# Sliding-window attention and a two-layer MLP: weights of a head in 192 columns, products with v as 128x64 and 64x64 tiles

## The chip, the cores and the metric

The kernel runs on one core of one Trainium2 chip. The metric is the device time of one execution in microseconds (us), as the median of several runs. A profiled execution has a time of its own; its span is what lies between its first and its last instruction. TensorE (PE in the profile) multiplies, VectorE (DVE) and ScalarE (ACT) work element by element, GpSimd (POOL) and SyncE (SP) mainly issue DMAs here. SBUF is the working memory with 128 partitions, PSUM the memory that TensorE writes.

## What is computed

```python
# q, k, v: (8, 8, 576, 64) = batch, heads, sequence, head_dim
def _attn_ref(q, k, v):
    window, scale = 128, 1.0 / np.sqrt(D)
    scores = scale * np.matmul(q, k.transpose(0, 1, 3, 2))
    rel = pos[:, None] - pos[None, :]
    slopes = 2.0 ** (-8.0 * (np.arange(H, dtype=np.float32) + 1) / H)
    bias = slopes[:, None, None] * (-np.abs(rel).astype(np.float32))[None, :, :]
    mask = (rel >= 0) & (rel < window)
    scores = np.where(mask, scores + bias[None], -1000000000.0)
    attn = softmax of scores over the keys
    return np.matmul(attn, v)

def _moe_ref(x, g_ln, w_ch1, w_ch2):   # x: (8, 576, 512), the heads side by side
    xn = (x - mu) / np.sqrt(var + 1e-06) * g_ln
    ch = np.maximum(xn @ w_ch1, 0.0) @ w_ch2      # 512 -> 2048 -> 512
    return (x + ch).astype(np.float32)
```

A query sees itself and the 127 keys before it. So a block of 128 queries needs two blocks of 128 keys, and of the 256 keys in them each query needs 128.

## The kernel before

**Blocks and order.** The batches are taken two at a time (four pairs, p = 0 to 3). The 576 tokens of a batch are four blocks of 128 and a tail of 64. A pair has nine slots: slot 2i + b is block i of its batch b, and slot 8 (`T`) is the two tails together, one batch on 64 partitions each. `order` lists the 36 slots; n is the place in it. Slots 0 and 1 see only their own keys, slots 2 to 7 those of slot blk - 2 and their own, slot 8 those of slots 6 and 7 and its own. The MLP works on groups of slots (`GROUPS`: 2, 2, 2, 2, then seven of 4).

**Two streams in one order.** `steps` (L740 to L794) is the list of attention steps. The MLP is a set of generators (`mlp1`, `mlp2`, `mlp2_seven`, `mlp1_last`, `mlp2_last`), and `weave_at` runs a given number of attention steps after given units of them. Each engine executes its instructions in the order in which they were written this way. For n from 8 on (L772 to L794) a slot has four steps: the first holds the masks and the products with v of slot n and one call of `attend` for slot n + 2 (or, if slot n + 1 is a tail, the tail's own-key call), the second the other calls, the third and fourth masks, squares and DMA transposes.

**Loads.** POOL issues the loads of q, k, v and the weights in the order of `loads` (L291 to L311), at most up to a given place (`load_until`). `load_v` (L283) makes one DMA per slot, two for a tail, into one of ten v buffers `vext`, [128 tokens, 8 heads, 64 + a column of ones]. From n = 13 on q and k are loaded as they lie (`load_natural`, L258; k one DMA for each batch, q two, even and odd tokens apart) and turned by DMA transposes that SP issues (`turn_natural`, L370). Before that, q and k are loaded with two tokens in a row (`load_qk`), turned by TensorE (`transposed`) and copied out of PSUM by DVE and ACT in `turn`, `turn_first` and `copy_second`. k's copy puts the tokens back in order and so writes with a stride; q's copy leaves the even tokens first and the odd ones behind, and writes in a row. Outputs are stored to even and odd rows by two DMAs (`store`, L1216).

**Scores.** `attend` (L469) computes transposed scores, keys on partitions and queries along columns, with K = 64 (head_dim) and 64 keys at a time, so each product uses a 64x64 quarter of the array; the two heads of a head pair hp use the two halves of the rows (j), the key halves c the two halves of the columns. `seen` (L443) leaves out those 64 keys by 64 queries that the window excludes, except in the first pair (`SEEN`). A call for two head pairs fills a pair of PSUM banks, [128 keys, 2, 2, 2 key blocks, 128 queries]; ACT takes the exponential (L504) into `probs`, 1024 columns at a time, and DVE multiplies by the decay mask (`masks`, L516). The masks `m_full`, `m_ends`, `m_tail` hold exp(-slope x distance), or 0 outside the window; ACT makes them from tables of distances (`decay`, L149). For slots 0 and 1 of the first pair TensorE adds the distances instead (`add_distances`). The tail has three calls: two for the keys of slots 6 and 7, one (`tail_attend`) for its own keys.

**Products with v.** In `values_at_once` (L571) each head and key block is one product with the weights [128 keys, 128 queries] stationary and 65 columns of `vext` moving, L579; for slots 2 to 7 that is 16 products, for the tail 24, for slots 0 and 1 eight. Slots 4 to 7 of the first pair do the same in two halves of four heads (`values`, L540, products at L550). The 65th column gives the sum of the weights. DVE divides by it (L587, L588; L558, L559), then `centre` subtracts the mean and the block goes into the MLP.

**The start.** The first steps turn the first slot by TensorE, with products on constants (`warm`) between. SP loads `first_tables` (the identity and two tables of distances) and the gains, POOL the first q and k, then v of slots 0 and 1, q and k of slot 2, the first quarter of w1, v of slots 2 and 3, the other quarters of w1 and two of w2.

Of the kernel before, what the change touches and what calls it, by code (L numbers as in the profile page):

```python
# [32 lines left out]
BY_DMA = SEEN = 8  # L33
# [38 lines left out]
def tables():  # L72

    key = np.arange(P)[:, None]
    query = np.arange(P)[None, :]

    def far(rel, ok=True):
        return np.where(ok & (rel >= 0) & (rel < WINDOW), rel, FAR)

    ends = [far(P + query - HALF * b - key, query // HALF == b) for b in range(2)]
    tail = far(query - key, query // HALF == key // HALF)
    evens_first = np.r_[0:P:2, 1:P:2]
    both = [far(P + query - key), far(query - key)]
    cols = [np.eye(P), *(m[:, evens_first] for m in both), *ends, tail]
    return np.concatenate(cols, axis=1).astype(np.float16)
# [3 lines left out]
def kernel(  # L93
# [21 lines left out]
    def pool(name, bufs, **kw):  # L115
# [22 lines left out]
    more_tables = consts.tile([P, 3 * P], FP16)  # L138
# [5 lines left out]
    m_full, m_ends = (  # L144
        consts.tile([P, H, 2 * P], FP16, name=f"m{i}", tag=f"m{i}") for i in range(2)
    )
    m_tail = consts.tile([P, H, P], FP16)

    def decay(m, heads=range(H)):  # L149

        n = m.shape[2]
        src = {id(m_full): first_tables[:, P:], id(m_ends): more_tables[:, 0 : 2 * P]}.get(
            id(m), more_tables[:, 2 * P :]
        )
        for h in heads:
            nc.scalar.activation(
                out=m[:, h, :],
                in_=src,
                func=AF.Exp,
                scale=-(2.0 ** (-8.0 * (h + 1) / H)),  # L160
            )
# [31 lines left out]
    def load_tables():  # L193
        nc.gpsimd.dma_start(out=more_tables, in_=tables_dram[:, 3 * P :])

    def slopes():

        for h in range(H):
            nc.vector.tensor_scalar(
                out=bias[:, h],  # L200
                in0=first_tables[:, 2 * P :],
# [56 lines left out]
    def load_natural(src, tag, p, i):  # L258
# [24 lines left out]
    def load_v(p, blk):  # L283
        vx = vext[(p * NSLOT + blk) % NV]
        for b, t0, n, p0 in spans(p, blk):
            nc.gpsimd.dma_start(  # L286
                out=vx[p0 : p0 + n, :, 0:D],
                in_=v[b, :, t0 : t0 + n, :].rearrange("h p d -> p h d"),
            )
# [59 lines left out]
    def turn(p, i, in_sc=False, copies=(nc.vector.tensor_copy, nc.scalar.copy)):  # L349
# [37 lines left out]
    def queries(p, i):  # L387
        t = turned_pool["q"].tile([P, 2, 2, HP, HALF], FP16, tag="q", name="q")
        turned["q", p, i] = t.rearrange("p b r h c -> p b h r c")
        return t  # L390

# [7 lines left out]
    def turn_first(b, copy):  # L399

        if b == 0:
            first_turned.extend((queries(0, 0), keys_tile("k", 0, 0)))
# [13 lines left out]
        nc.vector.tensor_copy(out=q[:, b], in_=ps[0])  # L416
        copy(out=k[:, b].rearrange("p h (c r) -> p r h c", r=2), in_=ps[1])
# [8 lines left out]
    def copy_second():  # L426

        q, k, ps = queries(0, 1), keys_tile("k", 0, 1), second_pair
        for t, b, copy in (
# [5 lines left out]
            dst = t[:, b] if t is q else t[:, b].rearrange("p h (c r) -> p r h c", r=2)  # L435
# [4 lines left out]
    def in_halves(t):  # L440
        return t if len(t.shape) == 3 else t.rearrange("p (r c) -> p r c", r=2)
# [880 lines left out]
```

## Time and profile before

| | |
|---|---|
| median of 3 runs | 308.59 us (308.33 to 309.37) |
| profiled execution | 307.95 us, span 306.2 us |
| granted TensorE clock | 0.993 of full speed |
| TensorE weight loads busy | 203.2 us (66%), beside the products |
| scores, L495 | 1088 products of 64x64 tiles |
| products with v, L579 and L550 | 480 and 64 of 128x128, 65 columns each |
| exponentials, L504 | 68 x 128x1024, 1.02 us each |
| masks, L516 | 66 x 128x1024, 0.68 us each |
| v loads, L286 | 40 issues on POOL, 34.1 us |
| natural q loads, L275 | 40 issues on POOL, 27.4 us |
| POOL's DMA queue | 103792 packets, 18.46 MB |
| HBM | read 36.90 MB, written 9.44 MB |

A row of the timeline gives the start of a run of like instructions, the time to the end of the last, the engine, the line of the kernel, the operation, what is written and read, the shape of the tile in the array, the moving operand and the count. TensorE's products overlap, so what a run costs is the distance from its start to the start of the next run. A row of waits names who waited for whom, the total, the number of times and the longest.

### The profile page before, as it was taken

How to read it: one execution, taken by the hardware profiler on the slowest of the kernel's cores; microseconds unless marked ns; L12 is line 12 of the kernel's file. 1: busy time of each engine (PE TensorE's matmuls, PEld its weight loads, DVE VectorE, ACT ScalarE, POOL GpSimd, SP SyncE). 2: the span in 40 equal slices, each digit the busy share in tenths (PEclk: the TensorE clock that was granted, in tenths of full speed). 3: DMA queues.
4: the chain of work that ended last, by engine and by line, in shares of the span. 5: the costliest groups of instructions: out<-in, count | busy, mean ns of one | idle time of the engine just before them, and what ended most of it. 6: DMA issues, size and time to landing. Idle time of an engine off the chain costs nothing.

```text
span 306.2 us, 9262 instructions
## 1 busy us (share of the span) xinstructions
PE 296.9 (97%) x3778; PEld 203.2 (66%) x3778; DVE 242.8 (79%) x646; ACT 181.7 (59%) x332; POOL 112.3 (37%) x153
## 2 busy tenths in 40 slices
PE   6899999999999999999999999999999999999994
PEld 2477755866755568646864686568656865698883
DVE  2588878779996799569967986798799878978983
ACT  5588776768966863675368635853586268506500
POOL 8933659763774372475107250760000000000000
PEclk9799999999999999999999999999999999999999
DMA  9999999999999999999999999999451043005014
GB/s 98 172 202 200 194 158 170 205 135 89 138 126 186 146 132 145 181 184 148 112 171 120 125 121 149 119 151 120 105 122 37 19 96 77 19 19 137 3 34 103
DMA packets 150074, 38.03 MB, mean 124 GB/s; under 512 B 140656, under 2 KB 145920, under 8 KB 150032
## 3 DMA queue, kind: packets, MB, share of 16 engines
q0 software_dynamic: 103792, 18.46, 96.0%
q1 hardware_dynamic: 45760, 18.60, 37.1%
q8 instruction: 29, 0.48, 0.7%
q10 hardware_dynamic: 480, 0.39, 0.5%
q14 instruction: 13, 0.11, 0.2%
HBM read 36.90 MB, written 9.44 MB: 151 GB/s over the span
## 4 chain that ended last, share of the span: by engine, by line
PE 91%; DMA 4%; ACT 1%; DVE 1%; POOL 1%; issue 1%; DVEq 0%; ACTq 0%; POOLq 0%
PE ps_m L832 35%; PE ps_s L1062 25%; PE ps_m L862 9%; PE ps_sc L495 6%; PE ps_sc L579 5%; PE ps_q L1141 4%; PE ps_x L956 3%; DMA q<-q 3%; DMA first<-in_k_dram 2%; PE ps_tr L343 1%; PE ps_warm L331 1%; POOL first L187 1%; PE ps_pv L550 1%; PE ps_tx L640 1%; PE ps_t L956 1%
## 5 line engine op out<-in xcount | busy, mean ns | idle before, releaser
L832 PE MATMUL ps_m<-xT,w1g 128*128 128x512 f16 (+1 forms) x512 | 103.7, 353 | 0.1
L848 ACT ACTIVATE ht_all<-ps_m 128x512 f16<-128x512 f32 (+1 forms) x143 | 71.5, 512 | 26.1 <-PE ps_m L832 24.0
L504 ACT ACTIVATE probs<-ps_sc 128x1024 f16<-128x1024 f32 x56 | 56.6, 1024 | 45.4 <-PE ps_sc L495 45.4
L832 PEld LDWEIGHTS <-w1g 128*128 128x128 f16 x512 | 47.7, 98 | 42.6 <-issue 0.3
L286 POOL DMA_DIRECT2D vx<-in_v_dram x40 | 34.1, 859 | 67.9 <-PE ps_sc L579 38.1
L1062 PE MATMUL ps_s<-w,s 128*128 128x256 f16 x384 | 43.8, 273 | 0.0
L1062 PEld LDWEIGHTS <-s 128*128 128x128 f16 x384 | 36.7, 98 | 4.7
L516 DVE TENSOR_TENSOR probs<-probs,m 128x1024 f16<-128x1024 f16 x56 | 36.9, 683 | 2.5 <-ACT probs L504 2.5
L1062 PE MATMUL ps_s<-w,ht_all 128*128 128x256 f16 x288 | 34.3, 273 | 0.0
L862 PE MATMUL ps_m<-w,ht_all 128*128 128x512 f16 x128 | 31.3, 380 | 0.0
L1062 PEld LDWEIGHTS <-ht_all 128*128 128x128 f16 x288 | 27.4, 98 | 4.9
L275 POOL DMA_DIRECT2D q<-in_q_dram x40 | 27.4, 697 | 6.0 <-DMA vx<-in_v_dram 2.2
L1083 DVE SCALAR_TENSOR_TENSOR o<-ps_s,rstd,x 128x256 f32<-128x256 f32 x48 | 21.0, 478 | 8.5 <-PE ps_s L1062 8.4
L882 DVE TENSOR_TENSOR s<-ht_all 128x1024 f16<-128x1024 f16 (+2 forms) x36 | 20.5, 571 | 7.9 <-ACT ht_all L848 6.7
L495 PE MATMUL ps_sc<-q,k 64*64 64x128 f16 (+1 forms) x1088 | 24.8, 212 | 0.6 <-ACT q L436 0.3
L495 PEld LDWEIGHTS <-k 64*64 64x64 f16 x1088 | 16.2, 108 | 13.2 <-issue 10.3
L588 DVE SCALAR_TENSOR_TENSOR x<-ps_sc,rec 128x512 f16<-128x512 f32 x32 | 22.1, 691 | 1.1
L272 POOL DMA_DIRECT2D k<-in_k_dram x20 | 17.9, 910 | 8.4 <-DMA k<-k 5.9
L664 ACT ACTIVATE junk<-xc 128x512 f16<-128x512 f16 x28 | 17.6, 628 | 5.7 <-DVE xc L620 5.6
L1083 DVE SCALAR_TENSOR_TENSOR o<-ps_s,rstd,o 128x256 f32<-128x256 f32 x36 | 15.7, 478 | 3.4 <-PE ps_s L1062 3.1
L579 PEld LDWEIGHTS <-probs 128*128 128x128 f16 x384 | 15.9, 98 | 3.6
L862 PEld LDWEIGHTS <-ht_all 128*128 128x128 f16 x128 | 11.1, 98 | 10.8
(117 smaller groups left out, 371.7 us busy)
## 6 DMA issues: line engine op xcount, KB each, us to landing
out_dram<-o SPq DMA_DIRECT2D x64, 128.0 KB, 2.5
vx<-in_v_dram POOLq DMA_DIRECT2D x32, 128.0 KB, 7.1
w<-in_moe_w_ch_dram POOLq DMA_DIRECT2D x8, 512.0 KB, 11.2
k<-in_k_dram POOLq DMA_DIRECT2D x30, 128.0 KB, 7.2
q<-in_q_dram POOLq DMA_DIRECT2D x48, 64.0 KB, 6.7
q<-in_q_dram POOLq DMA_DIRECT2D x10, 128.0 KB, 6.8
out_dram<-o SPq DMA_DIRECT2D x10, 64.0 KB, 1.9
k<-in_k_dram POOLq DMA_DIRECT2D x8, 64.0 KB, 7.7
```

What stands on the lines that cost most here:

```text
L275: nc.gpsimd.dma_start(out=t[half, b], in_=tokens.rearrange("h (c r) d -> r c h d", r=2)[r],)
L286: nc.gpsimd.dma_start(out=vx[p0 : p0 + n, :, 0:D], in_=v[b, :, t0 : t0 + n, :].rearrange("h p d -> p h d"),)
L495: nc.tensor.matmul(in_halves(ps[cols, j, n, t, :])[:, r, queries], kt[rows, hp, cols], in_halves(qt[rows, b, hp])[:, r, queries], start=no ...
L504: nc.scalar.activation(out=dst.rearrange("p (n j) q -> p j n q", j=2), in_=ps.rearrange("p j n t q -> p j n (t q)"), func=AF.Exp, scale=in ...
L516: nc.vector.tensor_tensor(out=dst, in0=dst, in1=mask, op=ALU.mult)
L579: nc.tensor.matmul(ps[:, h, 0 : D + 1], pr[:, h, t, :], vext[(p * NSLOT + o) % NV][:, h, :], start=(n == 0), stop=(n == len(terms) - 1),)
L588: nc.vector.scalar_tensor_tensor(out=x.rearrange("p (h d) -> p h d", h=H), in0=ps[:, :, 0:D], scalar=1.0, in1=rec.unsqueeze(2).broadcast_t ...
L832: nc.tensor.matmul(ps[:, 0:cols], w[:, kb, fb * P : (fb + 1) * P], xT[:, kb, 0:cols], start=(kb == 0), stop=(kb == NKB - 1),)
L848: nc.scalar.activation(out=ht[:, fb, :], in_=ps[:, 0:cols], func=AF.Relu)
L862: nc.tensor.matmul(sums[at], ht[:, fb, at * P : (at + 1) * P], w2[:, fb, :], start=(fb == 0), stop=(fb == NFB - 1),)
L1062: nc.tensor.matmul(ps[:, pair, :], lhs[:, fb, at : at + P], rhs[:, fb, :], start=(first and pair == 0 and fb == 0), stop=(fb == half - 1), ...
L1083: nc.vector.scalar_tensor_tensor(out=outs[at][:, cols], in0=ps[:, pair], scalar=rstd[:, n : n + 1], in1=(xs[p, blk] if fresh else outs[at] ...
```

## The change

The weights of a head for a slot with two key blocks take 192 columns in place of 256. A query of the first half of the block (early) needs all of the earlier block's second half, and parts of the earlier block's first half and of its own first half; one of the second half (late) needs all of its own first half, and parts of its own second half and of the earlier block's second half. The 192 columns are: all 128 earlier keys for the early queries (64 columns); 64 columns shared by two quarters, the own first half of the keys for the early queries on one half of the partitions and the earlier second half for the late queries on the other; the 128 own keys for the late queries (64 columns). The tail is put into 192 columns in the same way, with its own keys in the middle, so that it has two calls of `attend` and no third. For heads 4 to 7 the two halves of the partitions change places, in the scores, the masks and v.

`weigh` makes the products with v: for each head two of a 128x64 tile (all rows, 64 queries), then, all heads over again, two of a 64x64 tile for the middle columns. Slots 0 and 1 keep 128x128. `load_v` loads heads 0 to 3 as before, and heads 4 to 7 with the halves about, in two DMAs: three for a slot in place of one, four for a tail in place of two. Queries are in token order everywhere: q's copies write with a stride like k's, natural q is one DMA for each batch, and outputs are stored by one DMA for each slot, but for the last four. The scores in the first pair leave out what the window excludes, too. The masks' tables are now [identity, own and own turned about], [two and two turned about], [last and last turned about], of 96 KB each; SP loads the second right behind the first.

```diff
-BY_DMA = SEEN = 8
+BY_DMA = 8
...
+    early, late = query[:, :HALF], query[:, HALF:]
+    upper = key < HALF
+    def far(rel):
+        return np.where((rel >= 0) & (rel < WINDOW), rel, FAR)
+    own = far(query - key)
+    of_two = np.where(upper, early - key, P + late - key)
+    two = np.concatenate([far(P + early - key), far(of_two), far(late - key)], axis=1)
+    ahead = far(P + early - key)
+    last = np.concatenate([ahead, far(early - key % HALF), ahead], axis=1)
+    cols = [np.eye(P)]
+    for m in (own, two, last):
+        cols += [m, np.roll(m, HALF, axis=0)]
...
+    next_tables, more_tables = (
+        consts.tile([P, 6 * HALF], FP16, name=f"tables{i}", tag=f"tables{i}") for i in range(2)
+    )
...
-    m_full, m_ends = (
-        consts.tile([P, H, 2 * P], FP16, name=f"m{i}", tag=f"m{i}") for i in range(2)
+    m_two, m_last = (
+        consts.tile([P, H, 3 * HALF], FP16, name=f"m{i}", tag=f"m{i}") for i in range(2)
     )
-    m_tail = consts.tile([P, H, P], FP16)
-    def decay(m, heads=range(H)):
+    m_own = consts.tile([P, H, P], FP16)
+    def distances(m, h):
         n = m.shape[2]
-        src = {id(m_full): first_tables[:, P:], id(m_ends): more_tables[:, 0 : 2 * P]}.get(
-            id(m), more_tables[:, 2 * P :]
-        )
-        for h in heads:
+        src = {id(m_two): next_tables, id(m_last): more_tables}.get(
+            id(m), first_tables[:, P:]
+        )
+        return src[:, 2 * h // H * n : (2 * h // H + 1) * n]
...
-            if tag == "k":
-                nc.gpsimd.dma_start(out=t[:, b], in_=tokens.rearrange("h p d -> p h d"))
-            else:
-                for r, half in enumerate([slice(0, HALF), slice(HALF, P)]):
-                    nc.gpsimd.dma_start(
-                        out=t[half, b],
-                        in_=tokens.rearrange("h (c r) d -> r c h d", r=2)[r],
-                    )
+            nc.gpsimd.dma_start(out=t[:, b], in_=tokens.rearrange("h p d -> p h d"))
...
         vx = vext[(p * NSLOT + blk) % NV]
-        for b, t0, n, p0 in spans(p, blk):
-            nc.gpsimd.dma_start(
-                out=vx[p0 : p0 + n, :, 0:D],
-                in_=v[b, :, t0 : t0 + n, :].rearrange("h p d -> p h d"),
-            )
+        for heads, turned_about in ((slice(0, HP), False), (slice(HP, H), True)):
+            for b, t0, n, p0 in spans(p, blk):
+                tokens = v[b, heads, t0 : t0 + n, :].rearrange("h p d -> p h d")
+                if not turned_about:
+                    parts = [(p0, tokens)]
+                elif blk == T:
+                    parts = [(HALF - p0, tokens)]
+                else:
+                    parts = [(0, tokens[HALF:]), (HALF, tokens[:HALF])]
+                for at, src in parts:
+                    nc.gpsimd.dma_start(out=vx[at : at + src.shape[0], heads, 0:D], in_=src)
...
-            q = queries(p, i)
+            q = keys_tile("q", p, i)
             transposed("q", p, i, [t[:, 0] for t in ps])
             transposed("k", p, i, [t[:, 1] for t in ps])
             for b, copy in enumerate(copies):
-                copy(out=q[:, b], in_=ps[b][:, 0])
-                copy(out=k[:, b].rearrange("p h (c r) -> p r h c", r=2), in_=ps[b][:, 1])
+                for t, dst in enumerate((q, k)):
+                    copy(out=dst[:, b].rearrange("p h (c r) -> p r h c", r=2), in_=ps[b][:, t])
...
-        nc.vector.tensor_copy(out=q[:, b], in_=ps[0])
-        copy(out=k[:, b].rearrange("p h (c r) -> p r h c", r=2), in_=ps[1])
+        for t, src, copy in ((q, ps[0], nc.vector.tensor_copy), (k, ps[1], copy)):
+            copy(out=t[:, b].rearrange("p h (c r) -> p r h c", r=2), in_=src)
...
+    lower, upper, whole = slice(0, HALF), slice(HALF, P), slice(0, P)
+    def seen(blk):
         if blk == T:
-            batches = [slice(0, 1), slice(1, 2)]
-            return [(c, batches[c if o == T else t], every) for c in range(2)]
-        if o == blk:
-            return [(0, both, every), (1, both, second)]
-        return [(1, both, every), (0, both, first)]
+            turns = [(6, c, lower, 0) for c in range(2)] + [(7, c, upper, P) for c in range(2)]
+            return turns + [(T, 0, lower, HALF), (T, 1, upper, HALF)]
+        if blk < 2:
+            return [(blk, c, whole, 0) for c in range(2)]
+        return [
+            (blk - 2, 1, whole, 0),
+            (blk - 2, 0, lower, 0),
+            (blk, 1, upper, P),
+            (blk, 0, whole, HALF),
+        ]
...
+    def attend(p, blk, mask, tag, hps, sc=None):
         heads = slice(2 * hps[0], 2 * hps[-1] + 2)
-        nk = len(keys)
+        n = mask.shape[2]
         if hps[0] == 0:
-            pr = probs_pool.tile([P, H, nk, P], FP16, tag=tag, name=tag)
-            for t, o in enumerate(keys):
-                weights_of.setdefault((p, blk), []).append((pr, t, o))
-        else:
-            pr = weights_of[p, blk][-1][0]
+            weights_of[p, blk] = probs_pool.tile([P, H, n], FP16, tag=tag, name=tag)
...
+            for o, c, queries, col in seen(blk):
...
+                to = (lower, upper)[c ^ hp // 2]
+                for j in range(2):
+                    rows = slice(j * HALF, (j + 1) * HALF)
+                    nc.tensor.matmul(
+                        ps[to, j, at, col : col + queries.stop - queries.start],
+                        kt[rows, hp, c * HALF : (c + 1) * HALF],
+                        qt[rows, b, hp, queries],
...
-            return [(p, T, [6, 7], m_ends, "probs", hps) for hps in (low, high)]
         if blk < 2:
-            return [(p, blk, [blk], m_full[:, :, P:], "own", every)]
-        return [(p, blk, [blk - 2, blk], m_full, "probs", hps) for hps in (low, high)]
+            return [(p, blk, m_own, "own", every)]
+        return [(p, blk, m_last if blk == T else m_two, "probs", hps) for hps in (low, high)]
...
-    def tail_attend(p):
-        return (p, T, [T], m_tail, "own", [0, 1, 2, 3])
...
+    def weigh(p, blk, banks):
+        pr = weights_of[p, blk]
+        def value(o, h):
+            return vext[(p * NSLOT + o) % NV][:, h, :]
+        def product(j, n, half, rows, weights, o, first):
+            h = HP * j + n
+            nc.tensor.matmul(
+                banks[j][half, n, 0 : D + 1],
+                pr[rows, h, weights],
+                value(o, h)[rows],
+                start=first,
+                stop=True,
+                skip_group_check=True,
+            )
+        if blk < 2:
+            for n in range(HP):
+                for j in banks:
+                    product(j, n, whole, whole, whole, blk, True)
+            return
+        ahead, behind, halves = (6, 7, (T, T)) if blk == T else (blk - 2, blk, (blk, blk - 2))
+        for n in range(HP):
+            for j in banks:
+                product(j, n, lower, whole, slice(0, HALF), ahead, n == 0)
+                product(j, n, upper, whole, slice(P, P + HALF), behind, n == 0)
+        for n in range(HP):
+            for j in banks:
+                for c, (half, o) in enumerate(zip((lower, upper), halves)):
+                    product(j, n, half, (lower, upper)[c ^ j], upper, o, False)
...
+        ps = ps_mm.tile([P, HP, D + 1], FP32, tag="mm", name="ps_pv")
+        weigh(p, blk, {j: ps})
...
+        weigh(p, blk, {j: ps[:, j] for j in range(2)})
...
-    steps += [[(scores_tail, 0)] + scores_step(9) + masks_of(8) + masks_of(9)]
+    steps += [scores_step(9) + masks_of(8) + masks_of(9)]
...
-            todo.append(tail_attend(order[n][0]))
-        if n + 2 < count:
-            todo += attends(*order[n + 2])
+        todo = attends(*order[n + 2]) if n + 2 < count else []
...
+            if blk == T or two[0] is two[1]:
+                two[b % 2].dma_start(out=out[b, t0 : t0 + w, cols], in_=o[p0 : p0 + w, cols])
             else:
-                dst = dst.rearrange("(c r) d -> r c d", r=2)
                 for r in range(2):
-                    two[r].dma_start(
-                        out=dst[r], in_=src[r * HALF : (r + 1) * HALF]
-                    )
+                    rows = slice(r * HALF, (r + 1) * HALF)
+                    two[r].dma_start(out=out[b, t0:][rows, cols], in_=o[rows, cols])
...
+        nc.sync.dma_start(out=next_tables, in_=tables_dram[:, 3 * P : 6 * P])
```

Unchanged parts of functions, the renaming of `m_full` to `m_two` (or `m_own`) in `steps`, of `m_ends` to `m_last` and of `m_tail` to `m_own`, the division (now `divide`) and the other two calls that copy q are left out.

More of the change, by code (lines that the diff above doesn't have):

```diff
@@ L385, in bank @@
         )
[L387 to L390, printed above, removed]
     def keys_tile(tag, p, i):
@@ L401, in turn_first @@
         if b == 0:
-            first_turned.extend((queries(0, 0), keys_tile("k", 0, 0)))
+            first_turned.extend(keys_tile(tag, 0, 0) for tag in "qk")
         q, k = first_turned
@@ L543, in values, with divide @@
+    def divide(x, ps, rec, total):
+        nc.vector.reciprocal(out=rec, in_=ps[:, :, D])
+        nc.vector.scalar_tensor_tensor(
+            out=x.rearrange("p (h d) -> p h d", d=D),
+            in0=ps[:, :, 0:D],
+            scalar=1.0,
+            in1=rec.unsqueeze(2).broadcast_to([P, rec.shape[1], D]),
+            op0=ALU.mult,
+            op1=ALU.mult,
+            accum_out=total,
+        )
+    def values(p, blk, j):
+        if j == 0:
             xs[p, blk] = x_pool.tile([P, DM], FP16, tag="x", name="x")
@@ L571, in values_at_once @@
+        weigh(p, blk, {j: ps})
+        rec = small.tile([P, HP], FP32, tag="rec", name="rec")
+        x = xs[p, blk][:, j * HP * D : (j + 1) * HP * D]
+        divide(x, ps, rec, sums[p, blk][:, j : j + 1])
     def values_at_once(p, blk, sc=0):
```

118 lines of the change are left out of this document (21 added, 97 removed).

## The prediction

> **What bounds the kernel now.** I read the page's busy times first, then its waits, then TensorE's timeline in three places, then POOL's timeline at the start. The first two say who sets the end:
>
> ```profile
> PE 296.9 (97%) x3778; PEld 203.2 (66%) x3778; DVE 242.8 (79%) x646; ACT 181.7 (59%) x332; POOL 112.3 (37%) x153
> ...
> PE 91%; DMA 4%; ACT 1%; DVE 1%; POOL 1%; issue 1%; DVEq 0%; ACTq 0%; POOLq 0%
> ...
> POOL vx L286 <- PE ps_sc L579: 38.1, 8, 8.5
> POOL vx L286 <- PE ps_sc L495: 16.6, 3, 7.7
> ...
> PE ps_tr L411 <- DMA first<-in_k_dram: 1.9, 2, 1.2
> ```
>
> TensorE is busy 97% of the span and makes 91% of the chain that ended last. Its waits after the first 25 us are tenths of a us; POOL on the other hand waits 54.7 us in two rows for TensorE to free buffers. So the time is what TensorE has to issue, plus the start. ACT and DVE are not on the path: the exponentials (1.02 us each) and masks (0.68 us each) that become a quarter shorter give ACT some 56 x 0.2 = 11 us and DVE 56 x 0.12 = 7 us (a 128x768 sum takes 0.56 us), and I cost them at nothing, since TensorE waits for them nowhere that the sum can use.
>
> Now what a burst of small products costs on TensorE, from one start to the next:
>
> ```profile
> 58.66 0.41 PE L550 MATMUL ps_pv<-vx,probs 128*128 128x65 f16 x8
> 58.90 1.04 PE L832 MATMUL ps_m<-xT,w1g 128*128 128x256 f16 x8
> ...
> 119.94 0.65 PE L579 MATMUL ps_sc<-vx,probs 128*128 128x65 f16 x16
> 120.53 0.32 PE L495 MATMUL ps_sc<-q,k 64*64 64x64 f16 x16
> 120.78 1.92 PE L1062 MATMUL ps_s<-w,s 128*128 128x256 f16 x16
> ...
> 136.92 1.90 PE L832 MATMUL ps_m<-xT,w1g 128*128 128x512 f16 x8
> 138.75 0.37 PE L495 MATMUL ps_sc<-q,k 64*64 64x128 f16 x16
> 139.05 0.39 PE L832 MATMUL ps_m<-xT,w1g 128*128 128x512 f16 x1
> ```
>
> Eight whole-array products with v between products of the MLP: 0.24 us, 30 ns each. Sixteen followed by 64x64 products: 0.59 us, that is 16 x 30 ns = 0.48 and **0.11 us for the change of shape**. Into the scores: 136.92 + 8 x 0.216 (the usual distance of 512-column products: 4.32 us for 20 in the chain) = 138.65, but the scores start at 138.75, 0.10 us for the change. Sixteen 64-column scores took 0.25 us up to the MLP at 120.78; at 66.27, 32 of them followed by transposes of the same shape took 0.28 us, 9 ns each (four tiles at once), so 0.14 + 0.11 for the change back. Every change between 128x128 and 64x64 costs 0.10 us.
>
> **The change, part by part.**
>
> *Products with v.* A block with two key blocks goes from 16 whole-array products to 16 of 128x64 and then 16 of 64x64. No row shows 128x64. Bounds: two at a time as the 64x64 scores share the array (15 ns each) or one after another (30 ns). I take 15, since 64x64 tiles that share their rows run at once; 16 make 0.24 us. The 64x64 ones cost 9 ns, 0.14 us. Changes of shape: MLP to 128x64 is new, 0.10; 128x64 to 64x64 is new, bounds 0 and 0.10, I take 0.10 because every change of shape in the trace costs that; 64x64 to the scores behind is gone. Filling the array again costs some 0.02 us twice. So 0.10 + 0.24 + 0.10 + 0.14 + 0.02 = 0.60 where 0.59 was: **18 such blocks (pairs 1 to 3), +0.2 us**.
>
> The Trainium skill, "TensorEngine Tiling (Array Packing)", section Key Properties, says that changing the tiling mode, not just the tile, drains the engine; the 0.10 us rows agree. By that rule the step from 128x64 to 64x64 drains too, which is the end of the bounds that I took from the rows; without it the 32 places below would be 3.2 us cheaper.
>
> Where the products stand alone between MLP products, both the change in and the change out are new. Blocks 4 to 7 of the first pair are done in two halves, eight bursts of 0.24 us. After: 0.10 + 8 x 15 ns + 0.10 + 8 of 64x64 (a half uses two tiles at once, 18 ns each, 0.14) + 0.10 + 0.02 = 0.58. Six stand alone, +0.34 each; one has scores behind it (+0.15), one in front (+0.25): **+2.4 us**. Blocks 2 and 3 of the first pair: 0.10 + 0.24 + 0.10 + 0.14 + 0.10 + 0.02 = 0.70 against 0.51 and 0.48: **+0.4**. The last slot of a pair goes from 24 products (0.83 us, 129.04 to 129.87) to the same 0.60: 3 x -0.25; the last one of all stands alone, 0.73 to 0.68: **-0.8 in all**. In these 18 + 8 + 2 + 4 = 32 places the inner change of shape occurs once.
>
> *Scores.* The tail's own burst goes: 0.25 us with its change back, and the next burst moves up beside the products with v and loses its change in, 0.10; two bursts grow by 8 products of 9 ns. -0.21 for pairs 1 and 2, about 0 for the first and last: **-0.4**. In the first pair half the scores of blocks 2 to 7 shrink from 128 to 64 columns: 32 take 0.57 us (16.72 to 17.29), afterwards some 0.48, and 16 go from 0.35 to 0.32: **-0.5**. In pairs 1 to 3 the order within a head pair turns from 128, 64, 128, 64 to 128, 64, 64, 128 columns, so that the last 128-column score ends 64 columns later, 0.02 us x 36 bursts: **+0.8** (0 if TensorE fills the gap).
>
> Sum on TensorE: 0.2 + 2.4 + 0.4 - 0.8 - 0.4 - 0.5 + 0.8 = **+2.1 us**.
>
> *Copies of q.* They become strided like k's: DVE 0.42 to 0.72 us, ACT 0.59 to 0.74. The second one of the first block ends at 10.4 where scores start at 10.39: 0. ACT's copy at 16.08 is what TensorE waits for (0.33 us before 16.72): **+0.15**. The others lie beside MLP work; behind them on DVE and ACT wait masks and exponentials that TensorE needs later.
>
> *Loads.* A v load becomes three. An issue of 1024 pieces takes 0.86 us, of 512 pieces 0.70, of 256 pieces 0.58 (the tail's q: 1.16 for two). So v: 0.70 + 0.58 + 0.58 = 1.86, +1.0 x 32; tails +0.9 x 4; q in token order drops from four issues to two, -1.0 x 10. POOL gets +26 us, fewer than the 54.7 that it waits for TensorE. But not everywhere:
>
> ```profile
> 4.05 1.81 POOL L286 DMA_DIRECT2D vx<-in_v_dram  x2
> 5.80 1.43 POOL L251 DMA_DIRECT2D q<-in_q_dram  x2
> 7.15 1.44 POOL L251 DMA_DIRECT2D k<-in_k_dram  x2
> 8.48 0.86 POOL L212 DMA_DIRECT2D w<-in_moe_w_ch_dram  x1
> 9.23 1.87 POOL L286 DMA_DIRECT2D vx<-in_v_dram  x2
> 10.98 2.35 POOL L212 DMA_DIRECT2D w<-in_moe_w_ch_dram  x3
> ```
>
> The second quarter of w1 is issued at 10.98 and lands 9.6 us later, at 20.6; TensorE's first product with it starts at 20.60. There is no slack. Four v loads are ahead of it on POOL, so its issue slips 4 us. Most of the 9.6 us is queueing: a first q load landed in 3.8 us, pair 1's q in 5.0, so at q the queue holds 1.2 us of work when POOL brings 2 us of delay; the gap is 0.8 us. Bounds 0 (queue covers all) and +4.0 (all of it comes through). I take 0.8, less 0.3 that TensorE is itself late by then: **+0.5**. The new table on SP (96 KB like the first, which landed in 2.0 us) must be there before ACT's first masks; ACT idles 2.41 us behind those, so 0; without that cover the first k copy, and with it all, would be late. Its packets cost the first q and k at most 0.3 us. Later, POOL is dense from 44 to 68 us, and would be some 2 us late with k for pair 1's third block; SP, which turns it by DMA, has 3.5 us free before 74.82. 0, bound +2.
>
> *Stores* become one DMA in place of two on SP, 0.6 us saved each; nothing waits for them.
>
> **Sum:** 2.1 + 0.15 + 0.5 = +2.7 us, less some 0.1 us of waits (before the products at 20.09) that shorter masks take away: +2.6. The profiled execution takes 307.95 us, its span of 306.2 and 1.75 around it; 310.5 after. The median of the runs is 0.64 above the profiled one: **311.2 us**.
>
> **Rivals.**
>
> 1. *Not slower: going from 128x64 to 64x64 costs nothing*, since the columns stay split. For it: the trace shows no change of rows alone. Against: every change that it does show costs 0.10. Price: 32 x 0.12 (with its filling) = 3.8 us less, 307.4; it decides as soon as that step is below 0.04 us.
> 2. *Late loads.* If the first weights slip with POOL's whole delay, or the dense stretch makes the turned queries late: one on the chain landed 8.7 us after 77.47, and the scores at 86.18 started when it had. +1.5 to +4 us, 313.5. For it: w1's landing at the very moment of use. Against: POOL's long waits.
> 3. *Half-array products don't run two at a time.* 24 x 8 x 30 ns + 8 x 4 x 30 ns = +6.7, 318. Against: 64x64 tiles on the same rows do. The skill, same page, section Gotcha 2: Feature Incompatibilities, says column tiling excludes fast weight load; no row here shows that it hurts the 64x64 scores at 9 ns.
>
> **Chances.** Forecast 0.52 (309.5 to 312.7), rival 1 0.22, rival 2 0.19, rival 3 0.07. The range, 307.2 to 314.0, takes in the first three. Within 0.3% (0.9 us, about what can be told from no change) are a part of rival 1 and the low edge of the forecast: 0.14. Faster: most of rival 1, 0.19. Slower: 0.67.
>
> **What would show it.** In the profile after, the distance from the last 128x64 to the first 64x64 product (0.12 predicted, 0.03 by rival 1), 128x64 products starting in pairs some 30 ns apart, the lone half bursts at 0.58 us; DVE and ACT less busy by 7 and 11 us with no gain; w1's quarter landing near 21.4 with TensorE waiting some 0.5 us; POOL near 138 us. The prediction is wrong if full blocks take under 0.55 us on TensorE, or if TensorE shows waits over 1 us after the start.

## The result: 1.5% slower, and the profile after

| | before | after |
|---|---|---|
| median of the runs | 308.46 us (307.15 to 309.37, 4 runs) | 313.01 us (312.29 to 313.48, 4 runs) |
| profiled execution | 307.95 us, span 306.2 | 312.94 us, span 311.2 |

The ratio is 1.0149 (95% interval 1.0107 to 1.0191), +4.6 us (3.3 to 5.9), where +2.6 was forecast. Here and below the medians are over all runs, while a ratio, and a difference in us worked out from it, leaves out the few runs that were over 1.5% slower than the fastest of their kernel (one of `before_v3`, two of `before_v3late`, one of before).

The page of the kernel after, with the lines that answer to those shown of before (busy time, share and number of instructions for each engine; the chain that ended last; two groups of instructions):

```profile
PE 298.1 (96%) x4194; PEld 198.6 (64%) x4194; DVE 237.4 (76%) x642; ACT 168.2 (54%) x328; POOL 142.4 (46%) x205
...
PE 87%; DMA 5%; POOL 3%; DVE 2%; ACT 1%; issue 1%; ACTq 0%; POOLq 0%
...
L298 POOL DMA_DIRECT2D vx<-in_v_dram x112 | 74.1, 706 | 47.8 <-PE ps_sc L489 32.0
...
L498 ACT ACTIVATE probs<-ps_sc 128x768 f16<-128x768 f32 x56 | 44.7, 810 | 52.1 <-PE ps_sc L489 52.0
```

ACT gave back 13.5 us, DVE 5.4, and the end moved out. TensorE is 1.2 us busier, but the span grew by 5.0. In the chain DMA and POOL have 8%, where they had 5%. The waits of TensorE (total, times, longest) name the new one:

```profile
PE ps_m L823 <- DMA w<-in_moe_w_ch_dram: 4.0, 3, 1.7
```

Before had no such row. Where it arises stands in POOL's timeline (start, time to the end of the last, operation, count, in brackets the idle time ahead and what ended it), in after's:

```profile
4.04 4.02 POOL L298 DMA_DIRECT2D vx<-in_v_dram  x6
7.95 1.48 POOL L260 DMA_DIRECT2D q<-in_q_dram  x2
9.30 1.50 POOL L260 DMA_DIRECT2D k<-in_k_dram  x2
10.63 0.92 POOL L221 DMA_DIRECT2D w<-in_moe_w_ch_dram  x1
11.39 4.15 POOL L298 DMA_DIRECT2D vx<-in_v_dram  x6
15.39 0.89 POOL L221 DMA_DIRECT2D w<-in_moe_w_ch_dram  x1
19.25 1.50 POOL L221 DMA_DIRECT2D w<-in_moe_w_ch_dram  x2 [2.96 <-DMA w<-in_moe_w_ch_dram]
```

The quarters of w1 are issued at 10.63, 15.39, 19.25 and 20.0 (before: 8.48, 10.98, 11.72, 12.45). The third is held back for 2.96 us by another quarter's landing. The chain says which (start, length, what):

```profile
10.63 8.33 DMA w<-in_moe_w_ch_dram
18.96 0.28 issue
19.25 8.21 DMA w<-in_moe_w_ch_dram
27.46 0.05 issue
27.50 1.05 PE ps_m L823 x8
```

The first quarter lands at 18.96, only then is the third issued, and TensorE's third set of products waits until that has landed at 27.46. The chain doesn't say when the quarter would have landed if it had been issued sooner; the experiments do. TensorE's timeline, after and then before:

```profile
19.01 1.05 PE L823 MATMUL ps_m<-xT,w 128*128 128x256 f16 x8 [1.69 <-DMA w<-in_moe_w_ch_dram]
...
23.27 1.92 PE L823 MATMUL ps_m<-xT,w 128*128 128x256 f16 x16 [0.91 <-DMA w<-in_moe_w_ch_dram]
...
27.50 1.05 PE L823 MATMUL ps_m<-xT,w 128*128 128x256 f16 x8 [1.35 <-DMA w<-in_moe_w_ch_dram]
```

```profile
17.29 1.05 PE L832 MATMUL ps_m<-xT,w 128*128 128x256 f16 x8
...
20.60 1.92 PE L832 MATMUL ps_m<-xT,w 128*128 128x256 f16 x16
...
23.10 1.05 PE L832 MATMUL ps_m<-xT,w 128*128 128x256 f16 x8
```

The same products start 1.7, 2.7 and 4.4 us later. At the last product of the first pair's second layer (start at 97.94 us in place of 92.08) it is 5.9, and at the last product of all (306.93 in place of 301.80) 5.1: the later pairs give back 0.7.

Why the third quarter waits can be counted in POOL's rows. From its first DMA on, these are numbers 1 to 4 (first q, k), 5 to 10 (v), 11 to 14 (q, k), 15 (first quarter of w1), 16 to 21 (v), 22 and 23 (second and third quarter). Number 23 waits for number 15, the one eight before it. Before shows the same count where it cost nothing:

```profile
13.18 1.63 POOL L231 DMA_DIRECT2D w<-in_moe_w_ch_dram  x2
16.58 0.70 POOL L251 DMA_DIRECT2D q<-in_q_dram  x1 [1.77 <-DMA w<-in_moe_w_ch_dram]
17.57 0.68 POOL L251 DMA_DIRECT2D q<-in_q_dram  x1 [0.29 <-DMA vx<-in_v_dram]
```

There the first quarter is number 11 and landed at 16.3, and number 19, a load of q, is what waits for it. With two DMAs for v in place of six, all of w1 was issued ahead of that point.

### The profile page after: what moved, and what is told of

It reads as the page before. It is cut to its first block, busy times and chain, and to the rows that moved or that the text cites. A ratio compares the mean times of both kernels' runs of the same rounds, so it can differ in the third digit from the quotient of the medians.

```text
span 311.2 us, 10103 instructions
## 1 busy us (share of the span) xinstructions
PE 298.1 (96%) x4194; PEld 198.6 (64%) x4194; DVE 237.4 (76%) x642; ACT 168.2 (54%) x328; POOL 142.4 (46%) x205
## 4 chain that ended last, share of the span: by engine, by line
PE 87%; DMA 5%; POOL 3%; DVE 2%; ACT 1%; issue 1%; ACTq 0%; POOLq 0%
PE ps_m L823 35%; PE ps_s L1053 24%; PE ps_m L853 8%; DMA w<-in_moe_w_ch_dram 5%; PE ps_sc L538 5%; PE ps_sc L489 4%; PE ps_q L1132 4%; PE ps_x L947 3%; POOL vx L298 1%; PE ps_pv L538 1%; POOL first L196 1%; PE ps_s L947 1%; PE ps_t L947 1%; PE ps_tx L635 1%; ACT probs L498 0%
## 5 line engine op out<-in xcount | busy, mean ns | idle before, releaser
L298 POOL DMA_DIRECT2D vx<-in_v_dram x112 | 74.1, 706 | 47.8 <-PE ps_sc L489 32.0
L498 ACT ACTIVATE probs<-ps_sc 128x768 f16<-128x768 f32 x56 | 44.7, 810 | 52.1 <-PE ps_sc L489 52.0
L510 DVE TENSOR_TENSOR probs<-probs,m 128x768 f16<-128x768 f16 x56 | 29.5, 550 | 1.6 <-ACT probs L498 1.3
L1053 PEld LDWEIGHTS <-ht_all 128*128 128x128 f16 x288 | 27.4, 98 | 4.9
L489 PE MATMUL ps_sc<-q,k 64*64 64x64 f16 (+1 forms) x1088 | 22.5, 206 | 1.4 <-DVE k L421 0.7
L538 PEld LDWEIGHTS <-probs 128*64 128x64 f16 (+1 forms) x896 | 16.2, 108 | 11.8 <-issue 8.5
L489 PEld LDWEIGHTS <-k 64*64 64x64 f16 x1088 | 15.4, 107 | 11.7 <-issue 9.5
L280 POOL DMA_DIRECT2D q<-in_q_dram x20 | 18.1, 920 | 2.4 <-DMA k<-in_k_dram 1.7
L823 PE MATMUL ps_m<-xT,w 128*128 128x256 f16 x128 | 15.1, 273 | 4.0 <-DMA w<-in_moe_w_ch_dram 4.0
```

Of the source, the lines that this page charges most:

```text
L298: nc.gpsimd.dma_start(out=vx[at : at + src.shape[0], heads, 0:D], in_=src)
L489: nc.tensor.matmul(ps[to, j, at, col : col + queries.stop - queries.start], kt[rows, hp, c * HALF : (c + 1) * HALF], qt[rows, b, hp, queries],
L498: nc.scalar.activation(out=dst.rearrange("p (h j) q -> p j h q", j=2), in_=ps, func=AF.Exp, scale=inv_sqrt_d,)
L510: nc.vector.tensor_tensor(out=dst, in0=dst, in1=mask, op=ALU.mult)
L538: nc.tensor.matmul(banks[j][half, n, 0 : D + 1], pr[rows, h, weights], value(o, h)[rows], start=first, stop=True, skip_group_check=True,)
L823: nc.tensor.matmul(ps[:, 0:cols], w[:, kb, fb * P : (fb + 1) * P], xT[:, kb, 0:cols], start=(kb == 0), stop=(kb == NKB - 1),)
```

## The experiments

Theory A: the excess is the loads, at the start above all, since POOL needs longer to issue them and issues no DMA before the one eight earlier has landed. Theory B: it is TensorE's products and their changes of shape. Each kernel was timed beside the kernel before on the same chip.

| kernel | median us | before | ratio to before (95%) |
|---|---|---|---|
| `before_v3` | 314.77 | 308.76 | 1.0186 (1.0137 to 1.0236) |
| `before_v3_01` | 310.82 | 308.71 | 1.0080 (1.0053 to 1.0107) |
| `before_v3_23` | 308.61 | 308.71 | 0.9997 (0.9974 to 1.0020) |
| `before_v3late` | 309.81 | 308.22 | 1.0034 (1.0008 to 1.0060) |
| `after_v1` | 309.81 | 308.76 | 1.0035 (1.0008 to 1.0062) |
| `after_start1` | 309.49 | 308.22 | 1.0047 (1.0022 to 1.0071) |
| `after_v1_joint` | 308.72 | 308.22 | 1.0019 (0.9995 to 1.0043) |
| `after_w1two` | 312.23 | 308.76 | 1.0127 (1.0089 to 1.0164) |
| `after_lane` | 313.90 | 308.76 | 1.0166 (1.0135 to 1.0197) |
| `before_tail192` | 308.21 | 308.22 | 0.9991 (0.9968 to 1.0013) |
| the same again | 308.05 | 308.71 | 0.9974 (0.9949 to 0.9998) |

**The loads alone, in the kernel before** (`before_v3`). Every v load in three DMAs, none turned about, everything else as before:

```diff
-            nc.gpsimd.dma_start(
-                out=vx[p0 : p0 + n, :, 0:D],
-                in_=v[b, :, t0 : t0 + n, :].rearrange("h p d -> p h d"),
-            )
+            tokens = v[b, :, t0 : t0 + n, :].rearrange("h p d -> p h d")
+            nc.gpsimd.dma_start(out=vx[p0 : p0 + n, 0:HP, 0:D], in_=tokens[:, 0:HP])
+            for r in range(0, n, HALF):
+                nc.gpsimd.dma_start(
+                    out=vx[p0 + r : p0 + r + HALF, HP:H, 0:D],
+                    in_=tokens[r : r + HALF, HP:H],
+                )
```

> The kernel before, with only the v loads split as the change splits them: heads 0 to 3 in one DMA, heads 4 to 7 in two of 64 tokens, none turned about. Nothing else of the change. Theory A: the time was lost because POOL needs about 2 us per v load in place of 0.9, so that the quarters of w1 behind them land late (in the changed kernel TensorE waited 1.7, 0.9 and 1.35 us for them). Then this kernel loses about the same: 308.5 + 4 = 312.0 to 313.3 us, TensorE's waits for w near 4 us. Rival B: the added work on TensorE (lone half bursts, changes of shape) is the loss, and the waits for w only fill time that would be lost anyway: then this one stays at 308.3 to 309.5 us.

+5.7 us (4.2 to 7.3), above both forecasts and as much as the whole change or more: split loads alone can cost that much. These aren't quite the loads of the change, which also halves the issues of natural q. The profile, of the longest run (318.25 us), has a wait that the profile of after hasn't:

```profile
PE ps_sc L498 <- DMA q<-q: 4.6, 1, 4.6
PE ps_m L835 <- DMA w<-in_moe_w_ch_dram: 2.3, 2, 1.7
```

The first row is a wait at 95 us for q that SP turns by DMA; the second is the wait for w1 at the start.

**The change without its loads** (`after_v1`). One DMA for a slot of v, two for a tail. The v of heads 4 to 7 isn't turned about here (nor in `after_v1_joint`; in `after_start1` for four slots), so those heads multiply other rows of v; the number and shape of all instructions but the loads are unchanged.

> The changed kernel with one DMA per v slot as before (two for a tail); v of heads 4 to 7 is not turned about, so that their products with v take other values. Theory A: the waits for the quarters of w1 go, the third quarter's first product starts near 23.3 us as before (23.10) and not at 27.50, and the time falls to 308.3 to 309.3 us. Rival B: TensorE's added work remains, 310.5 to 311.5 us.

+1.1 us (0.25 to 1.9) is left of 4.6, between the two forecasts, so the loads cost some 3.5 us, all else 1.1. TensorE's wait for w1 shrinks to one row of 0.7 us.

**Where the loads cost it.** `after_start1` has one v DMA for slots 0 to 3 of the first pair only (`if p == 0 and blk < 4`), `before_v3late` the three for all slots but these.

> The changed kernel with one DMA each for v of slots 0 to 3 (their heads 4 to 7 not turned about, so their products take other values); all other v loads stay split. Theory A-start: the whole loss of the split loads is at the start, behind these four slots: the time equals that of the kernel with no split at all, 309.8 us (309.2 to 310.4), and TensorE's waits for w fall from 4.0 to 0.7 us. Theory A-both: later loads cost too (POOL dense from 44 to 68 us): 310.8 us or more, with a wait for the turned q or for v between 60 and 100 us.

> The kernel before with the v loads split from slot 4 on, slots 0 to 3 as they were. A-start: no loss, 308.3 to 309.4 us. A-both: with natural q still in two DMAs per batch, POOL has more to issue than in the changed kernel, and the turned q of pair 1's third block comes late (that wait was 4.6 us in the profile of the kernel with all v loads split): 311 to 314 us.

Undoing eight DMAs of the 112 takes 3.1 of the 4.6 us away (some 1.6 to 4.6 by the two intervals), as theory A-start forecast. Splitting v of the 32 other slots costs 1.0 us in the kernel before (interval 0.2 to 1.9), between the forecasts again. In the changed kernel `after_start1`, which keeps these, differs from `after_v1` by 0.4 us, less than the intervals.

**Which of the four slots.** `before_v3_01` splits v for slots 0 and 1 of the first pair alone, `before_v3_23` for slots 2 and 3 alone.

> The kernel before, with the v of slots 0 and 1 of the first pair alone loaded in three DMAs. Theory 'eight before' (a DMA of POOL's queue is issued only once the one eight before it has landed, and what is behind slots 0 and 1 in the queue is q1, k1 and the first quarter of w1): these are issued 2 us later (the first quarter at about 10.6 in place of 8.5), it lands near 18.9 in place of 16.3, TensorE waits some 1.7 us for it at the first MLP, and the later quarters cost no further wait: 308.2 + 1.7 = about 310 us (309.3 to 310.7). Rival 'every extra issue counts alike': half of what the six extra issues per slot pair cost at the start of before_v3, +2.3, 310.5 and as much in before_v3_23.

> The kernel before, with the v of slots 2 and 3 of the first pair alone loaded in three DMAs. Theory 'eight before': the first quarter of w1 is issued as before; the second is issued some 2 us later, which TensorE's work at the first MLP still covers; the third waits for the landing of the first until 16.3 and lands near 24.5, at the edge of being covered: 308.2 to 309.2 us, with at most 0.6 us of waits of TensorE for w. Rival 'every extra issue counts alike': 310.5.

+2.5 us (1.6 to 3.3) and -0.1 us (-0.8 to +0.6). So it isn't the number of issues: four more cost 2.5 us ahead of the first quarter of w1, and nothing behind it. The profile of `before_v3_23` shows in POOL's timeline what the theory asks for:

```profile
8.50 0.85 POOL L212 DMA_DIRECT2D w<-in_moe_w_ch_dram  x1
...
14.38 0.79 POOL L212 DMA_DIRECT2D w<-in_moe_w_ch_dram  x1
16.82 1.50 POOL L212 DMA_DIRECT2D w<-in_moe_w_ch_dram  x2 [1.65 <-DMA w<-in_moe_w_ch_dram]
```

The third quarter waits for the first here, too; but the first, issued on time, lands on time. Its second quarter was issued 3.4 us later than in before, and TensorE's products with it started 0.37 us later (20.97 for 20.60 us). TensorE waited 0.28 us for the second quarter and 0.79 for the third, 1.1 where at most 0.6 was forecast, and still no loss shows in the median. In `before_v3_01` the issue of the third quarter waits for nothing, as forecast (`w` x3 at 13.15), and TensorE waits 2.67 us for the first quarter and 0.28 for the second:

```profile
10.66 0.90 POOL L212 DMA_DIRECT2D w<-in_moe_w_ch_dram  x1
...
13.15 2.39 POOL L212 DMA_DIRECT2D w<-in_moe_w_ch_dram  x3
```

The two together (2.5 - 0.1) and the late ones (1.0) make 3.4, where all at once cost 5.7 (4.2 to 7.3). The gap isn't explained. It isn't seen at the start: by TensorE's products with the third quarter, the profile of `before_v3` is no later than that of `before_v3_01` (27.17 and 27.20 us; before 23.10), and TensorE doesn't wait for that quarter. What `before_v3` has on top is the wait of 4.6 us at 95 us; whether its other runs have it, no trace shows.

**Another order of loads.** `after_w1two` issues the second quarter of w1 right behind the first, ahead of v of slots 2 and 3; `after_lane` issues the first DMA of slot 2's v ahead of the first quarter, so that the third quarter has a DMA of v eight before it.

```diff
# after_w1two
-    weights = {3: w1s[1:] + w2s[:2], 4: w2s[2:], 5: [(load_tables,)]}
+    weights = {3: w1s[2:] + w2s[:2], 4: w2s[2:], 5: [(load_tables,)]}
-            loads += w1s[:1]
+            loads += w1s[:2]
# after_lane
-            loads += w1s[:1]
-        if n < V_FIRST:
+            loads += [(load_v, p, blk, 0)] + w1s[:1] + [(load_v, p, blk, 1)]
+        elif n < V_FIRST:
```

> The changed kernel with one place in the order of loads altered: the second quarter of w1 is loaded ahead of v of slots 2 and 3, right behind the first. Theory A: the two large loads give the queue work while POOL issues the six small ones. The first quarter lands as in the changed kernel (18.9 us, a wait of 1.7 us stays), the second some 2 us earlier and without a wait, the third near 25. 310.0 to 311.3 us. Rival B: under 0.7 us of gain, since the first quarter sets everything behind it.

> The changed kernel with the first quarter of w1 issued one DMA later, behind the first of the three DMAs of slot 2. POOL waited 2.96 us before it issued the third quarter at 19.25, until the first quarter had landed, and each POOL DMA seems to wait for the landing of the one eight before it. Theory A2 (that wait is a part of the loss): the third quarter now stands eight behind a small v DMA, is issued near 16.3, lands near 26 and not at 27.46, and 1 to 1.7 us are gained: 311.3 to 312.0 us, though the first quarter itself comes up to 0.7 us later. A1 (only POOL's own issue time matters): its landing stays near 27.4 and the time at 312.7 to 313.7 us.

Neither brought what theory A forecast. `after_w1two` is 0.8 us ahead by the medians and not 1.7 to 3.0, and the intervals overlap, so that no gain is shown. In its profile, the fastest of its six runs, the first quarter is issued at 10.63 as in after, but lands at 17.34 and not at 18.96, and TensorE doesn't wait for it; why isn't shown. TensorE's waits go over to v (`DMA vx`, 1.0 us at 20.7 and 21.5), with 0.5 us left for w1 at 25.49.

`after_lane` is no faster than after. The third quarter is issued at 16.02, 3.2 us sooner and without a wait; but it lands at 27.18, and in after it did at 27.46. That is the rival, A1, with its landing near 27.4 (its time, 312.7 to 313.7, is just exceeded). `before_v3_01` says the same: its third quarter is issued at 13.90 and lands at 27.16. So in these profiles the third quarter lands as late without that wait as with it. Whether the wait costs anything in after stays open, since the first quarter lands later in these two (20.75 and 19.59). What TensorE waits for in `after_lane` is the first quarter: issued 0.76 us later than in after, it lands 1.8 us later, at 20.75. The fourth, now the one with the first eight before it, is held back 4.05 us, and TensorE doesn't wait for it. POOL's and TensorE's timelines:

```profile
15.28 1.70 POOL L221 DMA_DIRECT2D w<-in_moe_w_ch_dram  x2
21.03 0.74 POOL L221 DMA_DIRECT2D w<-in_moe_w_ch_dram  x1 [4.05 <-DMA w<-in_moe_w_ch_dram]
```

```profile
20.80 1.14 PE L825 MATMUL ps_m<-xT,w 128*128 128x256 f16 x8 [3.52 <-DMA w<-in_moe_w_ch_dram]
21.86 0.54 PE L491 MATMUL ps_sc<-q,k 64*64 64x128 f16 x16
22.33 1.04 PE L825 MATMUL ps_m<-xT,w 128*128 128x256 f16 x4
23.30 0.53 PE L491 MATMUL ps_sc<-q,k 64*64 64x128 f16 x16
```

Behind the wait of 3.52 us four products take 0.97 us (22.33 to 23.30), where after had 0.54 (20.29 to 20.83): the granted clock, below.

**The halves joined** (`after_v1_joint`): `after_v1`, and slots 4 to 7 of the first pair make their products with v for all heads in one burst, not in two.

> The changed kernel with one DMA per v slot (heads 4 to 7 not turned about, other values) and the two halves of the products with v of slots 4 to 7 of the first pair put together: all 128x64 products of both halves, then all 64x64 ones. The lone halves cost 0.59 us each on TensorE by the profile, a change in, one inside and one out; together they need these once: 0.72 for both in place of 1.18. Theory B-part: what is left of the loss without the split loads (309.8 against 308.8) is these changes of shape: 4 x 0.45 = 1.8 us less, 307.9 to 308.5. Rival: two PSUM banks held at once make the MLP wait, or the path there is set by a DMA: 309.3 to 310.3 us.

308.72 us, just above the forecast of 307.9 to 308.5. Its profile starts the MLP within 0.04 us of that of `after_v1` and is 1.6 us ahead of it by the end of the first pair (last product of the second layer at 92.81 and 94.41 us). The ratios differ by 0.16%, less than their intervals, so the size rests on the profiles. With that, nothing measurable is left of the loss.

**The tail alone** (`before_tail192`): the kernel before, with only the last slot of each pair in 192 columns, two calls of `attend` in place of three, and nothing turned about.

```diff
-    ends = [far(P + query - HALF * b - key, query // HALF == b) for b in range(2)]
-    tail = far(query - key, query // HALF == key // HALF)
+    ahead = far(P + early - key)
+    last = np.concatenate([ahead, far(early - key % HALF), ahead], axis=1)
...
-        todo = []
-        if n + 1 < count and order[n + 1][1] == T:
-            todo.append(tail_attend(order[n][0]))
-        if n + 2 < count:
-            todo += attends(*order[n + 2])
+        todo = attends(*order[n + 2]) if n + 2 < count else []
```

> The kernel before with only the tail (slot 8) packed into 192 columns and nothing turned about, so that the loads stay as they were: two calls of attend for the tail and not three, 16 products of 128x64 and 16 of 64x64 (two at a time) in place of 24 of 128x128. My sum: the tail's products 0.83 to 0.75 us, its scores 0.21 less, four times: 308.8 - 1.1 = 307.7 us (307.2 to 308.3). Rival: no gain that can be told, 308.5 to 309.1, if the scores' next call does not move up without a stall for the PSUM banks.

> The same kernel as before_tail192, taken once more because its first interval holds both answers. By the stages of its profile it gains 0.87 us by the end of group 3 and 1.66 us by the end of the span: 307.2 to 308.0 us. Rival: those 1.6 us are within what one profile differs from the next, and the time is that of the kernel before, 308.2 to 308.6.

-0.3 us (-1.0 to +0.4) and -0.8 us (-1.6 to -0.1), where -1.1 was forecast at first. Its medians are the lowest of all kernels here; that it beats the one before is likely, not shown: the second interval just leaves out no change, the first doesn't. In the profile, pairs 1 to 3 give 0.8 us here (from 0.73 ahead at the last product of the first pair's second layer to 1.52 at the last of all), and 0.7 in `after_v1`. So all that packing gains there can be the tail's.

## Why the time came out higher than the sum, and inside the range

**The bound** was read rightly: ACT and DVE were relieved by 19 us, and the time shows no gain from it.

**Products with v.** Right, within hundredths. The page's timeline of after, a half burst between products of the MLP, and a full one:

```profile
59.41 0.60 PE L823 MATMUL ps_m<-xT,w1g 128*128 128x256 f16 x4
59.94 0.56 PE L538 MATMUL ps_pv<-vx,probs 128*64 128x65 f16 x16
60.43 1.81 PE L823 MATMUL ps_m<-xT,w1g 128*128 128x256 f16 x15
...
115.91 1.91 PE L1053 MATMUL ps_s<-w,ht_all 128*128 128x256 f16 x16
117.75 0.70 PE L538 MATMUL ps_sc<-vx,probs 128*64 128x65 f16 x32
118.27 0.36 PE L489 MATMUL ps_sc<-q,k 64*64 64x64 f16 x24
```

A product of 256 columns takes 0.109 us here, so the four end their part at 59.85; the half starts at 59.94 and the next product at 60.43: 0.09 + 0.49 = 0.58, as forecast. The sixteen end theirs at 117.66: 0.09 + 0.52 = 0.61, forecast 0.60. In single records of the trace the 128x64 products start in pairs some 30 ns apart, and from the last of them to the first 64x64 product it is 0.126 us, where 0.12 was forecast. With that rival 1 (no cost there, 0.03) and rival 3 (one product at a time) fall. With a burst of 16 scores behind it, a full block takes 0.895 us where it took 0.883: the row "18 such blocks, +0.2" holds, and packing a full block gains nothing on TensorE.

**The lone halves** (+2.4): `after_v1_joint` gets 1.6 us of it back with half the bursts, which agrees.

**Scores.** The +0.8 for the new order within a head pair wasn't there: in pairs 1 to 3, a burst of 16 scores between products of the MLP takes 0.302 us in both kernels. That is the case named beside it, "0 if TensorE fills the gap". The sum on TensorE becomes 1.3, and with +0.15 and -0.1 for the copies and waits 1.35; `after_v1` measured +1.1 (0.25 to 1.9).

**Loads at the start.** This is the term that was mis-sized: +0.5 was forecast, with 0 and +4.0 as bounds, and the runs give 3.1 (after against `after_start1`). Two things in its working failed, and a third was overlooked. First, it followed the second quarter of w1 alone. The first had 1.0 us of slack (landing 16.3, use 17.29) and two v loads ahead of it; its issue slipped 2.15 us, its landing 2.7, and TensorE waited 1.69. Even that slack is one profile's: in those of `before_v3late` and of the second `before_tail192`, whose loads start as in before, the first quarter lands at 15.78 and 16.08 and its first product starts at 16.39, so 0.6 and 0.3. Second, it took the queue to cover most of a late issue ("most of the 9.6 us is queueing"); `before_v3_01` shows 2.2 us of late issue cost 2.5 (1.6 to 3.3). Third, it priced the issues and not what holds an issue back: the third quarter was issued 7.5 us later than before, of which the extra issues explain 4.4 and the landing eight before it most of the rest. That wait stood four times in the trace of before, in the rows of POOL right below those quoted. What it costs isn't shown: without it, in `after_lane` and `before_v3_01`, the third quarter landed no more than 0.3 us sooner.

**Loads later.** Forecast 0, bound +2: `before_v3late` measured 1.0 (0.2 to 1.9), the changed kernel 0.4, which is within the intervals. The prediction named the place, q that SP turns by DMA: in the profile of `before_v3` TensorE waits 4.6 us for it. In those of after and of `before_v3late` it doesn't, so where the 1.0 us arises stays open.

So two errors of opposite sign, +0.8 that wasn't there and 2.6 us of loads too little, leave the time 1.8 above the forecast, outside the forecast's own band (309.5 to 312.7) and in the region of **rival 2**, "if the first weights slip with POOL's whole delay", 313.5. The range holds because it takes in that rival. The sign of being wrong that the prediction names, waits over 1 us after the start, shows too, if the start ends at 25 us as it says further up: TensorE waits 1.35 us before 27.50. The mechanism was named; its chance of 0.19 was too small, since the argument against it, POOL's long waits, belongs to a later stage than the one in which the weights are late.

## What to carry to other kernels

Work out a change of DMA count where a queue's order meets its first use: list for each transfer behind it the issue, the landing and the first use, and don't let slack in one stage pay for another. Count on a queue's rows which DMA each waiting issue waits for: an issue that waits for a landing some fixed number back slips with what is put between, even if the bytes are the same. Then read the landing as well; here the third quarter's landing hardly moved with its issue. Packing columns lowers the work of the engines that go over them, but pays on TensorE only where whole bursts or calls go away.

## What the hardware showed unasked

**The clock after a wait.** TensorE's granted clock fell to half behind some waits. Windows of `after_lane`, of after and of the second `before_tail192` (stretch in us, its length, busy time and count for each engine, granted TensorE clock, DMA share, GB/s):

```profile
20.80:23.00 2.20, 2.20 (x28) 1.47 (x28) 1.31 (x3) 0.55 (x1) 1.97 (x3) 0.69 1.28 207
23.00:25.00 2.00, 2.00 (x32) 1.05 (x32) 0.56 (x1) 1.62 (x4) 2.00 (x4) 0.50 1.24 205
```

```profile
19.00:21.60 2.60, 2.59 (x48) 1.78 (x48) 1.66 (x4) 1.19 (x3) 2.35 (x4) 1.00 1.10 162
```

```profile
21.80:24.80 3.00, 2.99 (x19) 2.24 (x20) 0.08 (x1) 1.16 (x3) 1.28 (x2) 0.61 1.25 207
```

Waits of 3.52 and 1.97 us were followed by a clock of 0.50 to 0.69 for 3 to 4 us, the one of 1.69 us in after by none. But length alone doesn't decide: in `before_v3` a wait of 1.68 us was followed by a clock of 0.59 and then 0.50, and eight products took 1.60 us where the same eight took 1.05 in after:

```profile
19.26 1.60 PE L835 MATMUL ps_m<-xT,w 128*128 128x256 f16 x8 [1.68 <-DMA w<-in_moe_w_ch_dram]
```

So a wait can cost more than its length: the profile of `before_v3_01`, the slowest of its nine runs, waits 2.67 us for the first quarter, runs at 0.56 to 0.66 until 24 us, and is 4.1 us behind before at the second quarter's products. The Trainium skill, "TensorE: Matmul & The Clock Gate", section What's actually happening, ties the half clock to a whole idle window of about 3.4 us; the wait of 3.52 us agrees, but here waits of 1.97 and 1.68 us were followed by it, too. It bears on single profiles more than on medians: that of the second `before_tail192` waited 1.97 us for the second quarter of w1, which was issued as in before, and took 309.47 where its median is 308.05.

**The start varies.** In kernels whose start is the same, the first MLP product of a profile came between 16.3 and 17.3 us. A difference of 1 us there, between two profiles, is no finding by itself.
